# An attention kernel's instruction order from a table of sequences instead of a list scheduler

## The chip, the core and the metric

The kernel runs on one core of a Trainium2 chip. The metric is the device time of one execution in microseconds, as the median of several runs. The engines of the core run their own instruction queues in program order and meet at semaphores: TensorE (PE in the profile, with PEld its weight loads), VectorE (DVE), ScalarE (ACT), GpSimd (POOL) and SyncE (SP), which here only issues DMA transfers.

## The reference

Two attention blocks over a sequence of 2048 tokens, width 1024, 32 heads of 32, are computed and concatenated. Block A is plain softmax attention:

```python
qkv = (lambda x, *d: x.transpose(*d))((x @ wqkv).reshape(B, S, 3, H, Dh), 2, 0, 3, 1, 4)
q, k, v = (qkv[0], qkv[1], qkv[2])
scores = jnp.einsum('bhqd,bhkd->bhqk', q, k) * Dh ** (-0.5)
p = _softmax(scores, axis=-1)
o = jnp.einsum('bhqk,bhkd->bhqd', p, v)
return (lambda x, *d: x.transpose(*d))(o, 0, 2, 1, 3).reshape(B, S, D) @ wo
```

Block B works on four segments of 512 tokens in turn: causal softmax attention inside the segment, and beside it a linear-attention read of a memory that the segments before have filled. The two are mixed by a sigmoid gate per head and projected by a matrix of its own. All inputs are bf16, and so is the output of 1 x 2048 x 2048.

## The kernel before

Everything is in SBUF once, and the work is cut into 11,109 small operations, each with its engine, its dependencies and an estimated duration. Python code plans them first and emits them afterwards, engine by engine, in the order that a scheduler found.

*Scores and exponentials.* Heads go in eight groups of four, queries in chunks of 256. A row of scores (`plan_set`, matmuls at L1271, 32-row tiles, so four heads at once) fills two of three PSUM slots of two banks each. There are 592 rows, numbered here 0 to 591 in the order in which they are planned; no change of order touches that. Each slot is then read by an exponential on ScalarE (`plan_exp`, L1347; the first eight, with a bias, L1334), which writes bf16 to a ring of 20 P buffers. For 238 slots ScalarE takes one bank only, and VectorE evicts the other (Y, L1308), whose square GpSimd makes (Pc, L1311).

*Values and sums.* P and Pc are multiplied with the values (L1438) and with ones for the softmax sums (L1445) on 32-column tiles. A group is four matmuls of 256 columns, which run side by side on four tiles. They accumulate in two pool banks. VectorE normalizes (L1504 to L1521), GpSimd multiplies (L1570), and the result goes out to be transposed by a DMA.

*Projections.* All projections are jobs (`plan_jobs`) of eight steps, issued by one helper (L899). A step is four matmuls of 512 columns. It exists as two halves of 256 columns; `join` makes one step of two halves that stand next to each other on TensorE's queue.

*Guards.* Before a group of heads is used for the first time a bound on its scores is worked out, since the exponentials are free of a running maximum: squares (GpSimd, L1672), sums on TensorE (L1685, L1715), a maximum on VectorE (L1692, L1719), a diagonal (L1702), its spreading on TensorE (L1762), and on VectorE L1770, `braw` (L1776), `bias` (L1789) and `flags` (L1783). ScalarE loads the flag and branches on it before the first exponential that relies on it. At a second guard of the same group L1736 keeps a running maximum, and L1742 is the exponential of a bias difference on ScalarE.

*The order.* `Prog.schedule` (L509 to L715) is a list scheduler. It keeps the ready operations of each engine and takes the next one in simulated time: on TensorE by a rank (`pick`) in which a score row goes first when it is due, a value group by its place relative to the exponentials opened so far, and a job by its due time; on the other engines by key. Some thirty constants weigh these rules, and the table `SHIFT` adds a correction to the key of hundreds of single items. It also chooses which of the two pool banks a value group or a job takes, and adds to large DMA transfers a dependency on an exponential that has ended. The queue that it builds is the program order of the engine.

Of the kernel before, what the change touches and what calls it, by code (L numbers as in the profile page):

```python
# [24 lines left out]
OL_LEAD, OL_MAX = 3.567283411686441, 21.60561264796846  # L25
# [14 lines left out]
SOON = 0.5969023125738563  # L40
# [88 lines left out]
class Op:  # L129
# [4 lines left out]
    def __init__(self, eng, fn, dur, lat, key, mode=None, sem=None):  # L134
# [16 lines left out]
SWITCH = 0.1  # L151
WIN = 3.413
ROW_LEAD = 5.053495059459838
AHEAD = 1.6055122421540051
HEAT = 8.05297032017043
STICK = 3.256770423473878
OVER = 17.394741454160474
PV_ROOM = 6.408007584666841
PV_T = 1.0806361081944706
PV_HOT = 1.0883878031673944  # L160
NORM_K = 6.738
JOB_AT = 1.5887710826754966
JOB_SLOPE = 1.1413237083257293
# [3 lines left out]
LEAD_A, LEAD_B, DUE_AT, DUE_SLOPE = 10.658, 3.249, 7.018517831572489, 1.9480960937294671  # L167
HOLD = {}
BACKLOG = 3.378
XR = 70.3728830950375  # L170
XC = 5.80397040345515
# [4 lines left out]
SAFE = 0.0  # L176
SHIFT = {((f, n), e): v for f, e, t in (
# [10 lines left out]
    ("plan_constants", "ACT", {  # L188
        1: 15.5}),
    ("plan_constants", "POOL", {  # L190
# [114 lines left out]
    ("plan_prologue", "PE", {  # L305
        2: 1.5, 5: -3.25, 6: 12, 7: 5, 8: 17.25, 9: 0.5}),
    ("plan_prologue", "POOL", {
        3: 5.5, 8: 0.5}),
    ("plan_prologue", "SP", {
        4: 13.47, 10: -1.78}),  # L310
    ("plan_pv", "DVE", {
# [2067 lines left out]
```

## Time and profile before

| | us |
|---|---|
| median of 3 runs | 1045.36 |
| lowest and highest | 1044.49, 1045.73 |
| span of the profiled execution | 1044.3 |
| TensorE busy | 1019.2 |
| ScalarE busy | 1016.3 |
| VectorE busy | 700.4 |
| GpSimd busy | 585.5 |

The profiled execution's own time is not listed apart from its span; the span leaves out about 1.1 us of what the median of the runs has. Start times are counted from the start of the span. In a row of the timeline the first number is the start, the second the duration, and the brackets hold the idle time of the engine just before and the operation whose end released it.

### The profile page before, as it was taken

The numbers are of one execution on the slowest core, as the hardware profiler recorded it, in microseconds if no ns is written. First come the engines' busy times: TensorE is split into PE (matmuls) and PEld (weight loads), VectorE is DVE, ScalarE is ACT, GpSimd is POOL, SyncE is SP. The second block draws the span as 40 slices with busy tenths as digits, with TensorE's granted clock in tenths as the row PEclk, the third lists the DMA queues.
The fourth block names the chain that finished last, engine by engine and source line by source line (L and its number), as shares of the span: only waits on it lengthen the run. The fifth ranks groups of instructions, "written<-read, shape, count | busy, mean of one in ns | idle before, by whom it ended". The sixth has DMA issues, their size and how long they took to land.

```text
span 1044.3 us, 56017 instructions
## 1 busy us (share of the span) xinstructions
PE 1019.2 (98%) x25384; PEld 559.9 (54%) x25385; DVE 700.4 (67%) x1559; ACT 1016.3 (97%) x1225; POOL 585.5 (56%) x677
## 2 busy tenths in 40 slices
PE   8999999999999999999999999999999999999998
PEld 4555555655555555565555545565555545455554
DVE  3366676767566686887865687687755885874444
ACT  5999989999999999999999999999999999999997
POOL 2125476668645675766656476665644775653310
PEclk9999999999999999999999999999999999999999
DMA  9042352124313331033223320133113561021101
GB/s 210 15 96 54 78 130 36 20 38 106 80 42 92 80 79 34 11 99 51 71 58 94 98 60 18 28 92 54 51 29 87 174 171 25 24 79 57 59 24 59
DMA packets 171390, 72.17 MB, mean 69 GB/s; under 512 B 134800, under 2 KB 169360, under 8 KB 171152
## 3 DMA queue, kind: packets, MB, share of 16 engines
q1 hardware_dynamic: 168784, 67.79, 26.7%
q8 instruction: 200, 3.28, 1.3%
q10 hardware_dynamic: 2368, 0.79, 0.3%
q14 instruction: 38, 0.31, 0.1%
HBM read 45.29 MB, written 11.73 MB: 55 GB/s over the span
## 4 chain that ended last, share of the span: by engine, by line
PE 66%; ACT 29%; DVE 3%; issue 1%; DMA 1%; POOL 0%; ACTq 0%; DVEq 0%
PE ps L899 32%; ACT P L1347 28%; PE ps L1271 13%; PE ps L1438 9%; PE ps L1445 9%; PE ps L1964 1%; DMA xT_A<-in_A_x_dram 1%; ACT PKQ_B L2008 1%; DVE Y L1308 1%; DVE T L1508 0%; PE ps L1715 0%; DVE OT_B L2035 0%; DVE T L1510 0%; DVE KQ_B L1658 0%; PE ps L1814 0%
## 5 line engine op out<-in xcount | busy, mean ns | idle before, releaser
L1347 ACT ACTIVATE P<-ps 128x1024 bf16<-128x1024 f32 (+1 forms) x1176 | 988.4, 1059 | 9.8 <-PE ps L1271 3.2
L1311 POOL TENSOR_TENSOR Pc<-Y 128x512 bf16<-128x512 f32 x238 | 249.4, 1049 | 257.2 <-PE ps L899 79.3
L1445 PE MATMUL ps<-P,onesb 128*32 128x256 bf16 (+1 forms) x4388 | 295.9, 270 | 0.8 <-issue 0.7
L1438 PE MATMUL ps<-P,V_A 128*32 128x256 bf16 x3620 | 252.7, 274 | 0.4 <-DVE V_A L1974 0.3
L1308 DVE TENSOR_SCALAR Y<-ps 128x512 f32<-128x512 f32 x238 | 163.4, 686 | 97.7 <-PE ps L1271 83.8
L1271 PE MATMUL ps<-KQ_A 32*128 32x256 bf16 x4096 | 204.0, 273 | 7.4 <-ACT P L1347 5.7
L1271 PEld LDWEIGHTS ps<-KQ_A 32*128 32x128 bf16 x4096 | 62.0, 92 | 154.0 <-ACT P L1347 111.7
L1445 PEld LDWEIGHTS ps<-P,onesb 128*32 128x32 bf16 x4388 | 128.8, 96 | 25.9 <-issue 12.9
L899 PE MATMUL ps<-xT_A,W_A 128*32 128x512 bf16 (+1 forms) x2236 | 138.8, 363 | 2.3 <-DMA xT_A<-in_A_x_dram 1.2
L899 PE MATMUL ps<-xT_B,W_B 128*32 128x512 bf16 (+1 forms) x2284 | 139.0, 359 | 1.2 <-DVE KQ_B L1658 0.3
L1438 PEld LDWEIGHTS ps<-P,V_A 128*32 128x32 bf16 x3620 | 107.7, 96 | 26.2 <-issue 10.9
L1438 PE MATMUL ps<-Pc,V_A 128*32 128x256 bf16 x476 | 119.5, 273 | 0.2
L1445 PE MATMUL ps<-Pc,onesb 128*32 128x256 bf16 x476 | 119.6, 274 | 0.0
L1370 POOL TENSOR_SCALAR_AFFINE_SELECT P<-P 128x768 bf16<-128x768 bf16 (+1 forms) x96 | 75.7, 794 | 49.9 <-ACT P L1347 48.3
L1672 POOL TENSOR_TENSOR sqA<-KQ_A 128x512 bf16<-128x512 bf16 x61 | 64.0, 1061 | 60.9 <-PE ps L899 31.5
L1672 POOL TENSOR_TENSOR sqB<-KQ_B 128x512 bf16<-128x512 bf16 x64 | 68.4, 1070 | 24.9 <-DVE KQ_B L1658 19.0
L899 PEld LDWEIGHTS ps<-xT_B,W_B 128*32 128x32 bf16 x2284 | 53.2, 96 | 46.6 <-issue 17.1
L899 PEld LDWEIGHTS ps<-xT_A,W_A 128*32 128x32 bf16 x2236 | 52.0, 96 | 48.7 <-issue 17.1
L1521 DVE STREAM_TRANSPOSE T<-rc 128x256 f32<-128x256 f32 (+1 forms) x152 | 72.3, 479 | 2.6
L899 PE MATMUL ps<-Wv_B,xT_B 128*32 128x512 bf16 (+1 forms) x1124 | 71.0, 362 | 0.8 <-issue 0.7
L1658 DVE CAST KQ_B<-ps 128x512 bf16<-128x512 f32 x64 | 44.1, 688 | 39.1 <-PE ps L899 38.4
L899 PE MATMUL ps<-Wo_B,OT_B 128*32 128x512 bf16 (+1 forms) x1112 | 68.6, 364 | 0.3 <-DVE T L1504 0.2
(117 smaller groups left out, 1224.5 us busy)
## 6 DMA issues: line engine op xcount, KB each, us to landing
Wv_B<-in_B_wv_dram SPq DMA_DIRECT2D x32, 256.0 KB, 3.3
W_B<-in_B_wk_dram SPq DMA_DIRECT2D x32, 256.0 KB, 3.4
W_B<-in_B_wq_dram SPq DMA_DIRECT2D x32, 256.0 KB, 4.0
Wo_B<-in_B_wo_dram SPq DMA_DIRECT2D x32, 256.0 KB, 3.3
out_dram<-outsb SPq DMA_DIRECT2D x56, 128.0 KB, 1.9
W_A<-in_A_wqkv_dram SPq DMA_DIRECT2D x14, 256.0 KB, 3.4
ot_a_scratch<-OTst SPq DMA_DIRECT2D x51, 64.0 KB, 1.8
xT_A<-ot_a_scratch SPq DMA_DIRECT2D x6, 512.0 KB, 4.9
```

The lines of the kernel that those rows point to most:

```text
L899: ins = e.matmul(out[r], w[:, r], x, start=start, stop=stop, tile_position=(0, 32 * t), skip_group_check=True)
L1271: ins = e.matmul(out, kap, qap, start=st, stop=True, tile_position=(32 * h, 0), skip_group_check=True)
L1308: o = self.dve(lambda e: e.tensor_scalar(Y[:, :], src, KAPPA * SCALE, BETA, ALU.mult, ALU.add), 512, key - 9.0, [self.bank[bank]], [rY], f ...
L1311: last.append(self.pool(lambda e: e.tensor_tensor(dst, Y[:, :], Y[:, :], ALU.mult), 512, key - BCK, [rY], [rP], rate=0.56))
L1347: a = self.act(guarded if early else lambda e: e.activation(dst, src, ACT.Exp, scale=SCALE), cols, key, rd, wr, fixed=EXP_FIXED + (0.095 i ...
L1370: self.pool(lambda e: e.affine_select(v, v, pattern=pat, compare_op=ALU.is_ge, fill=0.0, base=0, channel_multiplier=-1), 2 * nd * P, key + ...
L1438: ins = e.matmul(self.pb(obk, q0, q0 + nq, slice(32 * h, 32 * h + 32)), v, p, start=first, stop=last, tile_position=(0, 32 * h), skip_grou ...
L1445: ins = e.matmul(self.pb(obk, QC + q0, QC + q0 + nq, slice(32 * h, 32 * h + 32)), self.onesb[:, 0:32], p, start=False, stop=last, tile_pos ...
L1521: self.dve(lambda e: e.transpose(L2.rearrange("p (b r) -> p b r", r=32), bc), n, key, [rr], [rl], fixed=0.17)
L1658: self.dve(lambda e: e.tensor_copy(dst, src()), 512, key, [self.at(b)], rdst, fixed=0.155)
L1672: self.pool(lambda e: e.tensor_tensor(sq[:, :], src, src, ALU.mult), 512, key, [rsrc], [rs], rate=0.56)
L1964: o = self.pe(lambda e, i=i, t=t, k=k: e.matmul(self.pb(b, P * k, P * k + P), self.xT[:, i, P * t:P * t + P], self.WAv[:, i, P * half:P * ...
```

## The change

`SHIFT` and the constants of the list scheduler are gone. A table `ORDER` holds for each engine the sequence of its operations as pairs of a jump and a run length over the planned operations. `schedule` builds the queues from it and replays all engines to get start and end times, the pool bank that is free first and the dependencies of large transfers. One more line lets an exponential depend on the operation that writes its flag, which before only the branch did. The operations are the same. Behind the new function all lines have a number 27 or 28 higher than before (so L1271 is L1298 in the order after, L899 L926, L1438 L1466, L1445 L1473, L1789 L1817, L1783 L1811).

```diff
-SHIFT = {((f, n), e): v for f, e, t in (
-    ("load_OT_early", "SP", {
-        0: 5.57}),
...
+ORDER = {
+    "PE": (
+        25, 15, 13, 21, 7, 1, -8, 3, 117, 1, -111, 1, 3, 9, 118, 1, -119, 7, 118, 1, -105, 10, 7, 16, -23, 6, 114, 1,
...
     def schedule(self):
...
+        queue = {}
+        for e, runs in ORDER.items():
+            at, q = 0, []
+            for jump, n in zip(runs[::2], runs[1::2]):
+                at += jump
+                q += self.ops[at:at + n]
+                at += n
+            assert all(o.eng == e for o in q)
+            queue[e] = q
...
-        def pick(t, av, c):
-            mode = st["mode"]
-            row = [x for x in av if x.urgent]
...
+        def opening(b):
+            if holder[b] is not None and holder[b].left or not done.issuperset(last[b]):
+                return 1e9
+            return max((x.end + x.lat for x in last[b]), default=0.0)
...
+            for e, q in queue.items():
+                if at[e] == len(q):
+                    continue
+                o = q[at[e]]
...
+                if o.svc >= 0.8:
+                    was = next((x for x in reversed(progs) if x.end <= t), None)
+                    if was is not None:
+                        o.deps.add(was)
...
             if not early:
                 a.alt, a.flag = alt, self.flag_of[bc]
+                a.deps.add(a.flag[1])
```

Out of the longest common sequence of the two orders stand 957 operations of TensorE, 550 of VectorE, 267 of GpSimd, 175 of SyncE and 26 of ScalarE. Score rows and exponentials keep their own sequence. 117 steps more than before are issued as two halves, 468 matmuls more; changes of TensorE between 32-row and 32-column tiles are 1194 in place of 1198. The 238 evictions Y stand earlier in VectorE's queue, the normalizations later. Three places follow; in each row stand the line, the instruction, what it writes and reads, the size, and how many such instructions follow each other.

On VectorE, the guard of block B's first keys, at 142 us of the trace; T_2 is a normalization's tile and cu its correction. Before:

```order
L1464 TENSOR_SCALAR cu<-corr,flags 128x1 x2
L1719 TENSOR_REDUCE ps<-ps 128x1
L1702 TENSOR_SCALAR dg<-ps 128x32
L1770 TENSOR_REDUCE cols<-ps 128x2
L1776 TENSOR_SCALAR braw<-cols 128x1
L1504 TENSOR_TENSOR T_2<-ps,cu 128x512
L1789 TENSOR_SCALAR bias<-braw 128x1
L1783 TENSOR_SCALAR flags<-braw,flags 128x1
L1506 STREAM_TRANSPOSE T_2<-T_2 128x256
```

And after:

```order
L1534 STREAM_TRANSPOSE T_1<-T_1 128x256
L1547 RECIPROCAL rc<-T_1 128x8
L1747 TENSOR_REDUCE ps<-ps 128x1
L1730 TENSOR_SCALAR dg<-ps 128x32
L1798 TENSOR_REDUCE cols<-ps 128x2
L1804 TENSOR_SCALAR braw<-cols 128x1
L1817 TENSOR_SCALAR bias<-braw 128x1
L1811 TENSOR_SCALAR flags<-braw,flags 128x1
L1492 TENSOR_SCALAR cu<-corr,flags 128x1 x2
L1532 TENSOR_TENSOR T_2<-ps,cu 128x512
```

The subtraction into T_2 (L1504, now L1532) and the two corrections cu have moved behind the flag; two steps of another normalization now stand ahead of the guard.

On TensorE, from score row 182 on, around 327 to 332 us of the trace; KQ_A rows are score rows, xT_B,W_B and xT_A,W_A projection steps, P,V_A and P,onesb value and sum groups. Before (behind these rows come two more steps and four more groups, then row 185):

```order
L1271 MATMUL ps<-KQ_A 128x256 x8
L899 MATMUL ps<-xT_A,W_A 32x256 x4
L899 MATMUL ps<-xT_A,W_A 32x512 x16
L899 MATMUL ps<-xT_B,W_B 32x512 x20
L1271 MATMUL ps<-KQ_A 128x256 x8
L899 MATMUL ps<-xT_B,W_B 32x512 x24
L1271 MATMUL ps<-KQ_A 128x256 x8
L899 MATMUL ps<-xT_B,W_B 32x512 x12
L1438 MATMUL ps<-P,V_A 32x256 x4
L1445 MATMUL ps<-P,onesb 32x256 x4
```

And after, from row 182 to row 185:

```order
L1298 MATMUL ps<-KQ_A 128x256 x8
L926 MATMUL ps<-xT_A,W_A 32x512 x20
L926 MATMUL ps<-xT_B,W_B 32x512 x4
L1298 MATMUL ps<-KQ_A 128x256 x8
L926 MATMUL ps<-xT_B,W_B 32x512 x20
L1298 MATMUL ps<-KQ_A 128x256 x8
L926 MATMUL ps<-xT_B,W_B 32x512 x40
L926 MATMUL ps<-Wv_B,xT_B 32x256 x4
L1298 MATMUL ps<-KQ_A 128x256 x8
```

Each row from 183 on has fewer projection steps ahead of it, and the eight groups that stood between rows 184 and 185 have moved behind row 185.

On TensorE again, from row 433 to row 434, around 762 to 764 us. Before:

```order
L1271 MATMUL ps<-KQ_A 128x256 x8
L1438 MATMUL ps<-P,V_A 32x256 x4
L1445 MATMUL ps<-P,onesb 32x256 x4
L1438 MATMUL ps<-P,V_A 32x256 x4
L1445 MATMUL ps<-P,onesb 32x256 x4
L899 MATMUL ps<-xT_B,W_B 32x512 x8
L899 MATMUL ps<-xT_B,W_B 32x256 x4
L1271 MATMUL ps<-KQ_A 128x256 x8
L899 MATMUL ps<-xT_B,W_B 32x256 x4
L899 MATMUL ps<-xT_B,W_B 32x512 x20
```

And after:

```order
L1298 MATMUL ps<-KQ_A 128x256 x8
L926 MATMUL ps<-xT_B,W_B 32x512 x12
L926 MATMUL ps<-xT_B,W_B 32x256 x4
L1466 MATMUL ps<-P,V_A 32x256 x4
L1473 MATMUL ps<-P,onesb 32x256 x4
L1466 MATMUL ps<-P,V_A 32x256 x4
L1473 MATMUL ps<-P,onesb 32x256 x4
L926 MATMUL ps<-xT_B,W_B 32x256 x4
L926 MATMUL ps<-xT_B,W_B 32x512 x16
L1298 MATMUL ps<-KQ_A 128x256 x8
L1466 MATMUL ps<-P,V_A 32x256 x4
L1473 MATMUL ps<-P,onesb 32x256 x4
```

The whole projection job of eight steps now stands between the two rows, where two and a half of its steps did, and value groups follow row 434 at once.

More of the change, by code (lines that the diff above doesn't have):

```diff
@@ L166 @@
 RX0 = 34.374
[L167 to L168 removed]
+LEAD_A, LEAD_B = 10.658, 3.249
 BACKLOG = 3.378
[L170 to L171 removed]
 STEP = 1.599
@@ L549, in schedule @@
+        for q in queue.values():
+            for n, o in enumerate(q):
+                o.pos = n
+        for o in self.ops:
+            assert all(x.eng != o.eng or x.pos < o.pos for x in o.order)
+        at = dict.fromkeys(queue, 0)
+        free = dict.fromkeys(queue, 0.0)
+        ready = dict.fromkeys(queue)
         last = {b: list(r.w) + list(r.r) for b, r in self.before.items()}
         holder = dict.fromkeys(last)
-        st = self.st = dict(mode=None, prog=0.0, act_end=0.0, recent=[], win=0, acts={}, slow=0.0, opn=0, dma=0.0,
-                            rows=sum(o.urgent is not None and o.eng == "PE" for o in self.ops))
+        acts, win, low, mode, held, dma = {}, 0, False, None, 0.0, 0.0
@@ L559, in ready_of @@
                         (TO_POOL if o.eng == "POOL" and x.eng == "DVE" else 0.0) +
                         (TO_DVE if o.eng == "DVE" and x.eng == "PE" else 0.0))
-            for x in o.order:
-                t = max(t, x.start)
-            for x, w in o.gate:
-                t = max(t, x.end + x.lat - w)
-            return t
-        def past(t):
-            return next((x for x in reversed(queue["ACT"]) if x.prog and x.end <= t), None)
-        def opens(o):
-            return o.grp is not None and o is o.grp.pe[0]
```

235 lines of the change are left out of this document (46 added, 189 removed), and 666 rows, old and new, of tables (ORDER, SHIFT).

## The prediction

> **What bounds the kernel now.** I read the page first, then the waits of ScalarE, then ScalarE's busy time by stretch, then the timeline around each idle stretch that this showed.
>
> ```profile
> span 1044.3 us, 56017 instructions
> PE 1019.2 (98%) x25384; PEld 559.9 (54%) x25385; DVE 700.4 (67%) x1559; ACT 1016.3 (97%) x1225; POOL 585.5 (56%) x677
> PE 66%; ACT 29%; DVE 3%; issue 1%; DMA 1%; POOL 0%; ACTq 0%; DVEq 0%
> L1347 ACT ACTIVATE P<-ps 128x1024 bf16<-128x1024 f32 (+1 forms) x1176 | 988.4, 1059 | 9.8 <-PE ps L1271 3.2
> ```
>
> Two engines look full. The chain lies on TensorE for two thirds, but a full PE is modelled; what tells more is who waits. The exponentials (L1347) keep ScalarE busy for 988.4 us, and all its idle time in front of them is 9.8 us. TensorE's score rows (L1271) wait the other way:
>
> ```profile
> PEld ps L1271 <- ACT P L1347: 133.8, 416, 1.5
> PEld ps L1271 <- DVE Y L1308: 21.5, 67, 0.6
> ```
>
> So 483 times a row stood ready and its PSUM slot was not yet free. ScalarE sets the pace, and TensorE is a close second: 133.8/416 is 0.32 us a wait. Turning from the other tile shape costs 0.21 even for a row that waits for nothing:
>
> ```profile
> 333.50 0.12 PEld L1271 LDWEIGHTS ps<-KQ_A 32*128 32x128 bf16 x8 [0.21 <-issue]
> ```
>
> So a waiting row has on average about 0.1 us to spare. The change reorders the same work. It can give back ScalarE's idle time and no more, so I price it idle stretch by idle stretch. ScalarE's busy time by stretch, from the end of the start-up on:
>
> ```profile
> 24.00:140.00 116.00, 115.73 (x143) 1.00 0.31 66
> 140.00:145.00 5.00, 2.09 (x4) 1.00 0.56 168
> 145.00:333.00 188.00, 187.64 (x231) 1.00 0.29 67
> 333.00:335.00 2.00, 1.11 (x3) 1.00 0.00 0
> 335.00:396.00 61.00, 60.50 (x73) 1.00 0.30 73
> 396.00:398.00 2.00, 1.27 (x2) 1.00 0.34 66
> 398.00:765.00 367.00, 366.15 (x441) 1.00 0.25 59
> 765.00:767.00 2.00, 0.70 (x2) 1.00 0.00 0
> 767.00:1036.60 269.60, 268.64 (x321) 1.00 0.25 72
> 1036.60:1044.30 7.70, 1.20 (x2) 1.00 0.25 82
> ```
>
> Between 24 and 1036.6 us the idle time adds up to 0.27+2.91+0.36+0.89+0.50+0.73+0.85+1.30+0.96 = 8.77 us. The 7.7 us at the end are the last projection and its stores. The granted clock is 1.00 in every stretch, so no term hangs on the clock.
>
> The large ones by name, from the timeline (in brackets the idle time before the first exponential of a run):
>
> ```profile
> 143.82 1.02 ACT L1347 ACTIVATE P<-ps 128x1024 bf16<-128x1024 f32 x1 [2.91 <-PE ps L899]
> 333.95 1.94 ACT L1347 ACTIVATE P<-ps 128x1024 bf16<-128x1024 f32 x2 [0.89 <-PE ps L1271]
> 397.09 1.02 ACT L1347 ACTIVATE P<-ps 128x1024 bf16<-128x1024 f32 x1 [0.73 <-PE ps L1271]
> 766.46 2.43 ACT L1347 ACTIVATE P<-ps 128x1024 bf16<-128x1024 f32 x3 [1.30 <-PE ps L1445]
> 300.45 1.94 ACT L1347 ACTIVATE P<-ps 128x1024 bf16<-128x1024 f32 x2 [0.21 <-PE ps L1445]
> 760.90 4.26 ACT L1347 ACTIVATE P<-ps 128x1024 bf16<-128x1024 f32 x5 [0.18 <-PE ps L1271]
> ```
>
> These six are 6.22 us of the 8.77; the other 2.55 us are in small pieces.
>
> **The change, part by part.** *The guard at 143 us.* The first is no wait for a matmul, whatever the bracket says: ScalarE branches on a flag that VectorE writes at L1783.
>
> ```profile
> 142.30 0.21 DVE L1776 TENSOR_SCALAR braw<-cols 128x1 f32<-128x1 f32 x1
> 142.43 0.68 DVE L1504 TENSOR_TENSOR T<-ps,cu 128x512 f32<-128x512 f32 x1
> 143.03 0.21 DVE L1789 TENSOR_SCALAR bias<-braw 128x1 f32<-128x1 f32 x1
> 143.15 0.21 DVE L1783 TENSOR_SCALAR flags<-braw,flags 128x1 f32<-128x1 f32 x1
> ```
>
> The flag ends at 143.36, and the exponential follows 0.46 us later, after the flag is loaded and branched on. In the new order the 0.68 us subtraction (L1504) stands behind the flag. L1789 can then start 0.25 us behind L1776 (142.55; the same distance separates L1776 and L1783 in the next fence) and L1783 0.12 later, at 142.67 in place of 143.15: −0.5 us. Its bounds are 0, if TensorE or the transposes now put ahead of the chain hold it back, and −0.7, the whole subtraction.
>
> *The start.* The same chain for the second guard:
>
> ```profile
> 21.14 0.24 DVE L1702 TENSOR_SCALAR dg<-cols 128x32 bf16<-128x32 f32 x1
> 22.06 0.17 DVE L1770 TENSOR_REDUCE cols<-ps 128x2 f32<-128x16 f32 x1 [0.49 <-PE ps L1762]
> 22.27 0.21 DVE L1776 TENSOR_SCALAR braw<-cols 128x1 f32<-128x1 f32 x1
> 22.52 0.22 DVE L1783 TENSOR_SCALAR flags<-braw,flags 128x1 f32<-128x1 f32 x1
> 23.42 1.94 ACT L1347 ACTIVATE P<-ps 128x1024 bf16<-128x1024 f32 x2 [1.06 <-PE ps L1964]
> ```
>
> The diagonal is ready at 21.38, but VectorE waits 0.49 us for the spreading matmul L1762, which stands behind a score row; now it stands ahead of that row: −0.3. The bias (L1789) now comes before the flag: +0.13. The correction factor's exponential (L1742) moves from behind five exponentials into this wait, which costs nothing there. Together −0.2, bounds −0.5 and +0.3. Two weight loads go ahead of two transposing loads on SP's queue, and the transposes land later by them; ScalarE waits for neither here, so 0, and up to +1 if the projection behind them is.
>
> *Work moved behind rows that came late.* I count TensorE's work ahead of a row in the two orders and price it by the distance of starts on the full engine:
>
> ```profile
> 1035.00 0.28 PE L1438 MATMUL ps<-P,V_A 128*32 128x256 bf16 x4
> 1035.11 0.28 PE L1445 MATMUL ps<-P,onesb 128*32 128x256 bf16 x4
> 1035.22 1.04 PE L899 MATMUL ps<-V_A,xT_A 128*32 128x512 bf16 x16
> 1036.08 0.39 PE L899 MATMUL ps<-W_A,xT_A 128*32 128x512 bf16 x4
> 762.19 0.40 PE L1271 MATMUL ps<-KQ_A 32*128 32x256 bf16 x8
> ```
>
> A group of four 256-wide matmuls is 0.11; sixteen 512-wide ones take 0.65 longer than four, so a whole step of four is 0.22, and a half step 0.11. From row 182 to row 185, whose exponential is the one at 333.95, there were 20 steps, a half and eight groups, 5.4 us; now there are 21.5 steps, 4.7 us: −0.7, bounds 0 (VectorE's Y, which frees a slot there, stays as late) and −0.9. The same count for rows 220 to 223 gives −0.55 at 397.09 (bounds 0 and −0.7). At 766.46 the exponential waits until the value matmuls have read its P buffer. Work ahead of that last read is 0.4 less, and those eight groups now follow row 434 directly, so the read ends earlier still; but row 434 itself has 1.0 us more ahead of it, since seven steps and two halves now stand between rows 433 and 434 where there were two and a half. The old read and the new row then decide in turn; I take −0.5, bounds −0.9 and +0.4. The groups ahead of 300.45 and the row at 760.90 have 2.0 and 0.7 us less ahead, more than their idle time: −0.4 for both.
>
> *Small idle time.* Of the 2.55 us I take a third back, −0.9, my choice, since the trace does not say which of these rows had late work that moved; bounds 0 and −2.
>
> *Rows that get more work ahead.* By the same count nine rows have 0.3 to 1.0 us more: 434, 298, 304, 250, 187, 94, 516, 55 and 112, 5.7 us in all. A row is issued when the exponential of an earlier slot frees its banks; one more exponential (1.06 on the page) stands in front of ScalarE then, and the row takes 0.40, so 0.66 us is covered. Row 434 is in the term above already; 298, 304 and 250 (0.9, 0.8, 0.7) exceed it by 0.4 together, and I add as much again for rows whose cover is shorter: +0.8, bounds 0 and +4.6.
>
> *Steps issued in halves.* 117 more steps are issued as two 256-wide halves, 468 more matmuls, and changes between row and column tiles stay the same but for four. By the rows above two halves (2 × 0.11) take as long as a whole (0.22): 0. [...]
>
> *VectorE and GpSimd.* The 238 evictions Y (L1308) and their squares come earlier in their queues, the softmax normalizations later. What waits for the former is TensorE's row, which has its slot sooner; what waits for the latter is the output projection, far ahead of its due time. No idle stretch of ScalarE but 333.95 has such an end, so 0. The new dependency of exponentials on their flag adds no wait that the branch did not have. The end: the same projection steps behind the last exponential, one more value group of 0.11 beside them: 0.
>
> Sum: −0.5 −0.2 −0.7 −0.55 −0.5 −0.4 −0.9 +0.8 = −2.95. The profiled execution spans 1044.3 and its time lies beside the median of 1045.36 (1044.49 to 1045.73) with about 1.1 us outside the span: 1041.4 of span, 1042.4 us of time.
>
> **The rivals.** *The idle time only moves.* TensorE has little room, and work pushed behind row 185 stands in front of row 187, whose count rises by 0.6. For it: the 0.1 us of slack above. Against it: 483 rows still wait for a slot, so there is room a few rows on. Only the guards' −0.7 stay: 1044.7.
>
> *Slower: work ahead of just-in-time rows.* If the cover of 0.66 is not there, because a row's first exponential is the next that ScalarE takes, the nine rows' 5.7 us count from 0.1 of slack each: 5.7 − 0.9 = +4.8, and the gains from moved work go with it. 1045.4 − 0.7 + 4.8 = 1049.5. It decides from the point where a row starts more than 0.1 us behind the freeing of its slot; the 8 idle stretches behind L1271 that ScalarE shows in all of 592 rows speak against it:
>
> ```profile
> ACT P L1347 <- PE ps L1271: 3.2, 8, 0.9
> ```
>
> *Halves cost.* If each split leaves one weight load in the open, the row below gives 117 × 0.096 = 11.2 us of TensorE time, 1053.6 with the other terms, and less where rows wait anyway. The starts above speak against it.
>
> ```profile
> L899 PEld LDWEIGHTS ps<-xT_B,W_B 128*32 128x32 bf16 x2284 | 53.2, 96 | 46.6 <-issue 17.1
> ```
>
> [...]
>
> *All idle time goes.* The order is fitted closely enough that exponentials never wait after 24 us: 1045.4 − 8.8 = 1036.6. Against it, the guard at 143 keeps over two of them by the count above.
>
> *The table only restates the old order.* Excluded: 957 operations of TensorE and 550 of VectorE are out of the old sequence.
>
> **How the numbers follow.** Forecast 0.54, idle time only moves 0.24, slower 0.14, halves cost 0.03, all goes 0.05. The forecast is 1042.4 us. Its terms' bounds, not all at one end together, give about 1039.5 to 1045; the range reaches below for part of the case in which more idle time goes and above into the slower one: 1038.5 to 1047.5. A measurement of this kernel can tell about 0.2%, 2.1 us, from no change: faster is below 1043.3. Of the forecast's 0.54 some 0.46 lies there, with the 0.05 and 0.03 of the second case: 0.54. Slower than 1047.4: 0.14 and 0.03 less their mild part, 0.15. The rest, 0.31, is no difference.
>
> **What would show it.** In the profile after: the idle time before the exponential near 143 falls from 2.91 to about 2.4 with L1504 behind the flag; the stretches at 333, 397 and 766 fall to 0.2, 0.2 and 0.8; ScalarE's busy time stays 1016; four half-step matmuls stay 0.11 apart. Wrong would be: new idle stretches of over 0.3 us in front of rows 298, 304, 250 or 434 (the slower case), idle time of the same sum at other rows (it only moves), or more TensorE time in L899 with starts of halves over 0.12 apart.

## The result and the profile after

The kernel after takes 1057.57 us (median of 4 runs, 1053.38 to 1059.21), the one before 1045.55 beside it (1044.49 to 1045.76). The ratio is 1.0107, with a 95% interval of 1.0085 to 1.0128: slower by about 12 us, where 3 us less were forecast. The runs of the new order also lie further apart, 5.8 us against 1.3.

From the page of the kernel after, its span, the engines' busy time and the exponentials, whose line is now L1374:

```profile
span 1056.1 us, 56857 instructions
PE 1023.6 (97%) x25853; PEld 572.3 (54%) x25853; DVE 698.0 (66%) x1559; ACT 1017.2 (96%) x1225; POOL 584.4 (55%) x677
L1374 ACT ACTIVATE P<-ps 128x1024 bf16<-128x1024 f32 (+1 forms) x1176 | 987.8, 1056 | 20.3 <-PE ps L1298 14.9
```

ScalarE's work is the same, 987.8 us of exponentials against 988.4. Its idle time in front of them has more than doubled, 9.8 to 20.3. The table of waits says for whom (total, times, longest):

```profile
ACT P L1374 <- PE ps L1298: 14.9, 15, 5.2
PE ps L926 <- issue: 4.5, 4, 2.8
PE ps L926 <- DVE outsb L1686: 3.8, 1, 3.8
```

Score rows cost ScalarE 14.9 us where they cost 3.2. TensorE's projections (L926) waited once for 3.8 us for a cast of the output, a row that the table of before does not have. They also waited four times for nothing that the profile names ("issue"), 4.5 us in all and once for 2.8; before, that row was 1.0 us in two waits. ScalarE's busy time by stretch (length, then busy time and count, granted TensorE clock, share and rate of the DMA; the share adds up packets that overlap, so it can pass 1):

```profile
24.00:475.00 451.00, 444.25 (x539) 1.00 0.27 62
475.00:486.00 11.00, 6.59 (x9) 0.84 1.20 192
486.00:606.00 120.00, 120.00 (x147) 1.00 0.21 52
606.00:618.00 12.00, 5.38 (x7) 0.72 0.25 61
618.00:1047.90 429.90, 427.39 (x512) 1.00 0.25 68
```

Idle time from 24 us to the last exponential is 6.75 + 4.41 + 0 + 6.62 + 2.51 = 20.29 us; it was 8.77. The span is 24 us, 1003.62 of work, 20.29 idle and 8.2 behind it, 1056.1 in all; before, 24, 1003.83, 8.77 and 7.7. So the loss is idle time, and all but half a microsecond of it (11.03 of 11.52) lies in two stretches of 11 and 12 us. Outside them the new order is as good as the old one, not better.

**The places that the forecast named.** The timeline of the kernel after around 143, 333, 397 and 766 us (in brackets the idle time before the first of a run):

```profile
142.45 0.20 DVE L1811 TENSOR_SCALAR flags<-braw,flags 128x1 f32<-128x1 f32 x1
143.06 0.69 DVE L1532 TENSOR_TENSOR T<-ps,cu 128x512 f32<-128x512 f32 x1
143.14 4.69 ACT L1374 ACTIVATE P<-ps 128x1024 bf16<-128x1024 f32 x5 [2.10 <-DVE cu L1492]
333.23 3.52 ACT L1374 ACTIVATE P<-ps 128x1024 bf16<-128x1024 f32 x4 [0.26 <-PE ps L1298]
337.05 2.86 ACT L1374 ACTIVATE P<-ps 128x1024 bf16<-128x1024 f32 x3 [0.30 <-PE ps L1298]
396.36 10.38 ACT L1374 ACTIVATE P<-ps 128x1024 bf16<-128x1024 f32 x12
776.37 3.42 ACT L1374 ACTIVATE P<-ps 128x1024 bf16<-128x1024 f32 x4 [0.28 <-PE ps L1298]
```

The subtraction stands behind the flag, and 2.91 us have become 2.10. At 333 us 0.89 are 0.26; at 397 there is no idle time; the 1.30 at 766 are four pieces, none over 0.28. The second guard's exponential, at 23.42 us before, is at 22.56.

**The first new stretch, 475 to 486 us.** SP's queue, TensorE and ScalarE there (a row of SP's queue, SPq, is the issue on the engine, not the transfer):

```profile
469.39 6.11 SPq L1651 DMA_TRANSPOSE xT_B<-in_B_x_dram  x1
477.96 1.27 PE L926 MATMUL ps<-Wv_A,xT_A 128*32 128x256 bf16 x34 [2.78 <-issue]
480.68 1.51 ACT L1374 ACTIVATE P<-ps 128x512 bf16<-128x512 f32 x2 [3.46 <-PE ps L1298]
483.15 1.02 ACT L1374 ACTIVATE P<-ps 128x1024 bf16<-128x1024 f32 x1 [0.95 <-PE ps L1298]
```

TensorE stops for 2.78 us between the second and the third matmul of a step, where the profile names nothing that it waits for. A late block of its instructions fits this. The page counts the blocks of code that came in during the kernel:

```profile
q8 instruction: 203, 3.33, 1.3%
```

By this row they are 16.4 KB each (3.33 MB over 203), one about every 5 us; 51,706 matmuls and weight loads over 203 blocks are some 255 a block. The kernel before has 200 blocks for 50,769, some 254. In the DMA records of the trace one block starts at 467.58 us and the next only at 475.54. Between them lies the transposing load of x: its issue on SP runs from 469.39 to 475.50, and its data have landed at 479.09. TensorE had started 410 instructions since the last fetch when it stopped at 474.91; it goes on 2.4 us after the next one starts. In the old order SP issues the same load at 455.63, in front of four weight loads, with fetches at 455.14 and 460.88, and TensorE does not stop.

The clock falls behind the pause. TensorE by stretch, the granted clock ahead of the DMA's two columns:

```profile
478.00:480.00 2.00, 2.00 (x50) 0.72 1.32 259
480.00:482.00 2.00, 2.00 (x34) 0.50 1.33 223
482.00:484.00 2.00, 2.00 (x52) 0.93 0.95 181
```

The columns are averages over 2 us. The trace has a clock of either 1.0 or 0.5, and it is halved from 478.88 to 482.29 us, 3.41 us. A pause of 2.78 us and that stretch together became 4.41 us on ScalarE. In e2 and e4 below, pauses of 1.71 and 1.98 us were followed by the same 3.41 us at half clock. The length of the pause does not decide it alone: in e8 one of 2.26 us at 489.67 us was followed by full clock.

**The second, 606 to 618 us.** The cast of one output tile on VectorE, SP's queue up to its store (L2119), then VectorE, TensorE and ScalarE:

```profile
542.86 0.69 DVE L1686 CAST outsb<-ps 128x512 bf16<-128x512 f32 x1 [1.70 <-PE ps L1466]
601.54 2.66 SPq L1651 DMA_TRANSPOSE PKt_B<-PKQ_B  x1
605.34 0.58 SPq L2119 DMA_DIRECT2D out_dram<-outsb  x1
609.47 0.69 DVE L1686 CAST outsb<-ps 128x512 bf16<-128x512 f32 x1 [4.65 <-DMA out_dram<-outsb]
610.22 0.83 PE L926 MATMUL ps<-xT_B,W_B 128*32 128x512 bf16 x8 [3.83 <-DVE outsb L1686]
612.50 1.02 ACT L1374 ACTIVATE P<-ps 128x1024 bf16<-128x1024 f32 x1 [5.21 <-PE ps L1298]
615.88 2.43 ACT L1374 ACTIVATE P<-ps 128x1024 bf16<-128x1024 f32 x3 [1.42 <-PE ps L1473]
```

This is a chain over four engines. The output tile that was cast at 542.86 us is stored only at 605.34, 62 us later, because the new order puts its store that far back on SP's queue, behind loads, a transposing load and a store of OTst. In the order before, the store of the same tile follows its cast, which ends at 538.06, at once:

```profile
538.09 0.62 SPq L2091 DMA_DIRECT2D out_dram<-outsb  x1
```

There are three outsb buffers. In the new order the next cast into this one, at 609.47 us, waits 4.65 us until the store has landed, at 609.45. That cast holds a PSUM bank, TensorE waits 3.83 us for the bank, and the rows behind it come 5.21 us late. The clock is halved here as well, from 608.59 to 615.41 us.

### The profile page after: what moved, and what is told of

Read it like the earlier page. It is cut to its first block, busy times and chain, and to the rows that moved or that the text cites. A ratio compares the mean times of both kernels' runs of the same rounds, so it can differ in the third digit from the quotient of the medians.

```text
span 1056.1 us, 56857 instructions
## 1 busy us (share of the span) xinstructions
PE 1023.6 (97%) x25853; PEld 572.3 (54%) x25853; DVE 698.0 (66%) x1559; ACT 1017.2 (96%) x1225; POOL 584.4 (55%) x677
## 3 DMA queue, kind: packets, MB, share of 16 engines
q1 hardware_dynamic: 168784, 67.79, 26.5%
q8 instruction: 203, 3.33, 1.3%
## 4 chain that ended last, share of the span: by engine, by line
PE 59%; ACT 34%; DVE 2%; DMA 2%; issue 2%; POOL 0%; SPq 0%; ACTq 0%; DVEq 0%
ACT P L1374 34%; PE ps L926 29%; PE ps L1298 12%; PE ps L1466 9%; PE ps L1473 8%; PE ps L1992 1%; DMA W_B<-in_B_wq_dram 1%; DMA xT_A<-in_A_x_dram 1%; DVE Y L1335 1%; ACT PKQ_B L2036 1%; DMA out_dram<-outsb 0%; PE ps L1743 0%; DVE PKQ_B L2042 0%; DVE T L1536 0%; DVE outsb L1686 0%
## 5 line engine op out<-in xcount | busy, mean ns | idle before, releaser
L1374 ACT ACTIVATE P<-ps 128x1024 bf16<-128x1024 f32 (+1 forms) x1176 | 987.8, 1056 | 20.3 <-PE ps L1298 14.9
L1473 PE MATMUL ps<-P,onesb 128*32 128x256 bf16 (+1 forms) x4388 | 300.6, 271 | 0.1
L1466 PE MATMUL ps<-P,V_A 128*32 128x256 bf16 x3620 | 259.1, 275 | 0.1
L1298 PE MATMUL ps<-KQ_A 32*128 32x256 bf16 x4096 | 204.4, 273 | 8.2 <-ACT P L1374 4.0
L926 PE MATMUL ps<-xT_B,W_B 128*32 128x512 bf16 (+1 forms) x2356 | 145.3, 356 | 7.3 <-DVE outsb L1686 3.8
L926 PE MATMUL ps<-xT_A,W_A 128*32 128x512 bf16 (+1 forms) x2408 | 146.1, 349 | 1.3 <-DMA xT_A<-in_A_x_dram 0.9
L1298 PEld LDWEIGHTS ps<-KQ_A 32*128 32x128 bf16 x4096 | 62.0, 92 | 152.6 <-ACT P L1374 103.1
L1473 PEld LDWEIGHTS ps<-P,onesb 128*32 128x32 bf16 x4388 | 129.1, 97 | 25.3 <-issue 13.1
L1466 PEld LDWEIGHTS ps<-P,V_A 128*32 128x32 bf16 x3620 | 107.8, 96 | 29.4 <-issue 12.2
L1466 PE MATMUL ps<-Pc,V_A 128*32 128x256 bf16 x476 | 121.0, 274 | 0.0
L1473 PE MATMUL ps<-Pc,onesb 128*32 128x256 bf16 x476 | 120.7, 274 | 0.1
L926 PEld LDWEIGHTS ps<-xT_B,W_B 128*32 128x32 bf16 x2356 | 55.6, 96 | 52.3 <-issue 20.3
L926 PEld LDWEIGHTS ps<-xT_A,W_A 128*32 128x32 bf16 x2408 | 57.4, 96 | 43.5 <-issue 16.4
L926 PE MATMUL ps<-Wv_B,xT_B 128*32 128x512 bf16 (+1 forms) x1200 | 74.3, 351 | 0.4 <-DVE T L1532 0.3
L926 PE MATMUL ps<-Wo_B,OT_B 128*32 128x512 bf16 (+1 forms) x1220 | 72.7, 346 | 0.1
L1686 DVE CAST outsb<-ps 128x512 bf16<-128x512 f32 x56 | 38.4, 686 | 50.1 <-PE ps L926 28.4
```

What stands on the lines that cost most here:

```text
L926: ins = e.matmul(out[r], w[:, r], x, start=start, stop=stop, tile_position=(0, 32 * t), skip_group_check=True)
L1298: ins = e.matmul(out, kap, qap, start=st, stop=True, tile_position=(32 * h, 0), skip_group_check=True)
L1374: a = self.act(guarded if early else lambda e: e.activation(dst, src, ACT.Exp, scale=SCALE), cols, key, rd, wr, fixed=EXP_FIXED + (0.095 i ...
L1466: ins = e.matmul(self.pb(obk, q0, q0 + nq, slice(32 * h, 32 * h + 32)), v, p, start=first, stop=last, tile_position=(0, 32 * h), skip_grou ...
L1473: ins = e.matmul(self.pb(obk, QC + q0, QC + q0 + nq, slice(32 * h, 32 * h + 32)), self.onesb[:, 0:32], p, start=False, stop=last, tile_pos ...
L1686: self.dve(lambda e: e.tensor_copy(dst, src()), 512, key, [self.at(b)], rdst, fixed=0.155)
```

## The experiments

Theory A: SP's new order of DMA issues, which the forecast had priced at nothing, makes both stretches. Its rivals: B, the new function itself (its choice of PSUM banks and its added dependency) costs the time whatever the order is; C, the added halves cost it; D, TensorE has no room, and idle time taken away at one row comes back at others. Several edits below move one issue (or operation) in front of another, just ahead of the numbering of the queues, in this form:

```diff
+        for e, o, x in (("SP", 5786, 6516),):
+            q = queue[e]
+            q.remove(self.ops[o])
+            q.insert(q.index(self.ops[x]), self.ops[o])
```

**e1, the old order as a table.** The new function, with the table filled from the sequences that the old scheduler made.

> The order of before on all five engines, put into the new table and replayed by the new function. Theory A (two stalls that come from SyncE's new order of DMA issues): 1045 us, within 1 us of before, since SyncE's order is the old one. Rival B (the new function itself costs: its choice of pool banks, the added dependency of exponentials on flags): 1050 us or more with the old order too.

1046.66 us (1044.76 to 1047.82), ratio 1.0011 (1.0001 to 1.0020), span 1044.5. By the interval B costs 0.1 to 2.1 us, 1.0 by the medians of the ratios, and falls as the cause of 12: the loss is in the order.

**e2, the load of x ahead of the weight loads; e3, the output store put out earlier; e4, both.** The edits are the form above with ("SP", 4957, 5088), with ("SP", 5786, 6516), and with both.

> The changed kernel with one DMA issue moved: the transposing load of block B's third segment (469.39 in the profile after) goes ahead of the four value-weight loads and the store that stood before it, as it stood before the change. Theory A (TensorE's code fetch is held up by that transposing load when it comes on top of the loads): no idle stretch near 480, its 3.46 and 0.95 us go, about 1053 us. Rival C (the code is longer by 468 matmuls and its fetches run dry by themselves): the stretch stays or comes back nearby, 1057 us.

> The changed kernel with one DMA issue moved: the output store of 605.34 goes four places ahead, before the load and the transpose at 601. Theory A (VectorE's cast at 609 waits for that store, TensorE for the cast): the idle stretches of 5.21 and 1.42 us at 612 and 616 go, about 1051 us. Rival D (the cast waits for something else that the profile puts on the store, or another store is next): 1055 us or more.

> The changed kernel with both moves. Theory A: both stalls gone, 11 us less than the profile after, 1046 to 1047 us: what is left is the new order of the computing engines alone, whose gains and losses in the profile after nearly cancel. Rival E (the computing engines' order costs by rows that come just in time): 1050 us or more.

e3: 1050.95 (1050.36 to 1052.91), ratio 1.0045 (1.0028 to 1.0062), 6.6 us below the kernel after by the medians, about what the stretch held. ScalarE in e3 over the same two places:

```profile
470.00:490.00 20.00, 18.25 (x23) 1.00 0.97 188
604.00:628.00 24.00, 23.73 (x29) 1.00 0.55 136
```

One store moved four issues up leaves 0.27 us of idle time where 6.62 were. The chain from the store to the row is shown. That the two figures agree to 0.1 us is in part chance: the profiled run of e3 is its slowest, its span is 4.9 us below that of the kernel after, and it has more idle time and work elsewhere.

e2 is a miss: 1060.63 (1056.08 to 1063.94), ratio 1.0137 (1.0101 to 1.0172), no faster than the kernel after. So is e4: 1052.30 (1050.71 to 1054.24), ratio 1.0057 (1.0037 to 1.0077), where 1046 to 1047 were expected. The pause for code did not go, it moved. In e4:

```profile
458.75 4.51 SPq L1655 DMA_TRANSPOSE xT_B<-in_B_x_dram  x1
466.42 0.19 PE L1794 MATMUL ps<-pick,dg 128*32 128x16 bf16 x4 [1.98 <-issue]
467.69 2.02 ACT L1378 ACTIVATE P<-ps 128x1024 bf16<-128x1024 f32 x2 [1.63 <-PE ps L1302]
```

In e2 fetches start at 456.67 and 463.34 us, with the load between them from 458.13 to 462.59 and 425 instructions started meanwhile; TensorE then stops for 1.9 us. So the load's place ahead of the weight loads is not enough: there, too, a fetch comes late beside it.

**e6, no transposing load there; f3, the load late in the old order.** e6 is e3 with the third load of x brought in as one plain block of 128 KB; the other three quarters of it are left out. f3 is the old order with the load moved behind the four weight loads, where the new order has it.

```diff
+        if s == 2:
+            self.dma(lambda e: e.dma_start(self.xTB[:, 0, :], xb[L * s:L * s + P, 0:L]), ...
+            return
         self.turn(self.xTB[:, :, :], xb[L * s:L * s + L, :], self.sm_xTB, key, [], [self.r_xTB], 5.0, 3.4, True)
```

> The changed kernel with the output store moved ahead as in the run before, and the transposing load of block B's third segment replaced by a plain load of 128 KB into the same tile, so that segment is computed from mostly stale input. Theory A (the transposing load holds up TensorE's code fetch): the fetch after 470 comes within 5 us of the one before, the idle stretches of 1.33 and 0.26 us near 481 go, 1049 to 1050 us beside 1051 for the store move alone. Rival C (the code is too dense there whatever the DMA does): a pause of TensorE of 1.5 to 3 us near 478 stays.

> The old order with one DMA issue moved: the transposing load of block B's third segment goes behind the four value-weight loads that it stood before. Theory A: it takes 5 to 6 us in place of 3.8 and holds the code fetch so long that TensorE pauses 1 to 3 us near 465 to 475; 1046.5 to 1049 us. Rival G (the pause needs the new order's denser code): no pause over 0.7 us there, 1045 to 1046 us.

e6: 1049.50 (1048.39 to 1051.18), ratio 1.0039 (1.0026 to 1.0052). Its medians do not tell it from e3, but its profile shows the place. ScalarE in e6:

```profile
24.00:470.00 446.00, 438.68 (x531) 1.00 0.26 60
470.00:490.00 20.00, 19.92 (x26) 1.00 0.65 142
490.00:1038.40 548.40, 545.77 (x655) 1.00 0.24 65
```

With the transposing load gone the fetch comes in time, and 0.08 us are left of e3's 1.75. This fits theory A and does not prove it: in g2 and g3 below, with the load where e3 has it, only 0.34 and 0.54 us are left there. The block is also a plain load with a quarter of the bytes, so e6 could not tell transposing from bytes. f3: 1045.42 (1044.32 to 1048.39), ratio 1.0004 (0.9995 to 1.0013). In it the load runs from 466.99 to 472.47, a fetch starts at 469.12 and is not held, and TensorE does not stop. So the late load alone is harmless here. Which fetches are held beside such a load and which pass, the runs do not settle: in g2 and g3 fetches started 3.25 and 3.43 us behind its issue, and TensorE has no pause of over 0.41 us there.

**e5, more halves in the old order; f2, halves rejoined in the new.** e5 leaves 237 whole steps of the old order as halves, 948 matmuls more, twice what the change adds. f2 is e3 with 237 split steps joined.

```diff
+        apart = {self.ops[n] for n in APART}
...
-            if a.both is not None and a.both[0] is b:
+            if a.both is not None and a.both[0] is b and a not in apart:
```

> The old order on every engine, with the 237 steps that the change splits issued as two halves each: 948 matmuls more, twice the net of the change, and nothing moved. Rival C (halves cost TensorE time, 0.1 us a split): 1045 and up to 24 us more, with starts of halves over 0.12 us apart. Theory A (two halves take as long as a whole; they only make the code longer): 1045 to 1047 us, starts 0.11 apart, and pauses of TensorE without a semaphore only where a transposing load falls together with dense code.

> The changed kernel with the output store moved ahead, and in the 237 steps that the change splits the second half moved up to stand right behind the first, so that they are issued whole: 948 matmuls fewer. Theory A with the code's density as part of it (shorter code gives the fetch more time): the pauses at 477 and 876 shrink, 1048 to 1050 us beside 1051. Rival F (the halves are placed where they fit, and work that moves up makes rows late): 1052 us or more.

e5: 1048.47 (1046.45 to 1049.67), ratio 1.0024 (1.0015 to 1.0033), 1.8 us over e1 by the medians. f2: 1051.08 (1050.70 to 1051.83), ratio 1.0058, no better than e3. The change's 468 matmuls would thus cost about 0.9 us by e5, and f2 could not show even that. C falls as the cause. Over 948 matmuls e5's 1.8 us would be an estimated 1.9 ns each. The runs do not tell that from the cost of the more code that e5 fetches, an estimated seven blocks (1,896 matmuls and weight loads at 255 a block).

**e7 and e8, one engine's queue from the other order.** e7 has the new order with SP's old sequence, e8 the old order with SP's new one. The queues would block each other, so 38 and 14 of SP's issues are taken out of turn.

> The new order on the four computing engines with SyncE's old order, in which 38 issues are taken out of turn where the new order of the others needs it. Theory A (what is lost comes from SyncE's issues): no stall on the output store at 606, pauses of TensorE's code fetch as before the change or shorter, 1045 to 1048 us. Rival E (the computing engines' new order loses by itself): 1050 us or more with no wait for a DMA. Some of the issues taken out of turn may wait themselves; the trace shows it then as a wait for a load.

> The old order on the four computing engines with SyncE's new order, in which 14 issues are taken out of turn. Theory A: slower than before by stalls on DMA or on the code fetch, 1050 us or more. Rival E (SyncE's order does not matter): 1045 to 1047 us.

1148.74 us (ratio 1.0996) and 1063.97 (ratio 1.0171, 1.0156 to 1.0187). e7 misses the 1045 to 1048 us expected of it by 100 us; e8 falls on the side of theory A. Both are confounded by the issues out of turn and separate nothing; they show the price of a misfit. In e8 stores of OTst wait on SP's queue, GpSimd waits for their buffers, and an exponential at 152.82 us for 10.8 us:

```profile
POOL OTst L1581 <- DMA ot_a_scratch<-OTst: 29.2, 7, 9.6
ACT P L1357 <- DVE cu L1475: 10.8, 1, 10.8
```

**f1 and f4, the new order in front, the old behind.** f1 takes the new order to 75 us and the guard's subtraction behind its flag, f4 the new order to 440 us; the tables are spliced there.

> The new order of all engines for what starts in the first 75 us, the old order from there on, and of the later changes one alone: at the guard of 143 us VectorE's subtraction (L1504) stands behind the flag. The profiles show exponentials 0.8 to 1.5 us earlier at 70 us in the new order, and the guard's idle stretch 0.7 us shorter. If both hold by themselves: 1043.5 to 1044 us, 1.5 to 2 us faster than before. If an idle stretch only moves: 1045 to 1046.

> The new order of all engines for what starts in the first 440 us, the old order from there on: it has the guard, the rows of 333 and 397 and the start, and neither stall. The forecast's terms for this part are 0.5, 0.2, 0.7, 0.55 and half of the 0.4, some 2.1 us: 1043.5 us. If the idle time only moved: 1045 to 1046.5 us.

1049.10 (ratio 1.0039, 1.0026 to 1.0052) and 1051.15 (ratio 1.0069, 1.0051 to 1.0088). Both miss, since the splice itself waits: idle stretches of 1.95 and 0.71 us at 83 and 85 us in f1, of 2.32, 0.78 and 0.68 at 455 to 460 in f4. What the new order does ahead of the splice is better read in the kernel after itself. From 24 to 400 us, the kernel before, the kernel after and f4:

```profile
24.00:400.00 376.00, 370.36 (x453) 1.00 0.30 68
24.00:400.00 376.00, 370.35 (x452) 1.00 0.29 67
24.00:400.00 376.00, 368.64 (x449) 1.00 0.29 68
```

The gains at 143, 333 and 397 us are in it, and the new order has 5.65 us of idle time there against 5.64: what it wins by then it has also lost. The 7.36 us of f4 have in them what a pause of TensorE for code cost, 1.22 us at 209.44, which the kernel after does not have there.

**g1, three of the forecast's moves alone in the old order.** The subtraction behind its flag, row 185 ahead of the work that stood before it, and the value groups of 766 us half a job forward.

```diff
+        for e, o, x in (("DVE", 1578, 1579), ("PE", 3664, 3620), ("PE", 8240, 7801), ("PE", 8241, 7801), ...
```

> The old order, with three of the moves that the forecast counted on and nothing else: VectorE's subtraction (L1504) behind the flag at 143 us, row 185 ahead of the two groups and five steps of work that stood in front of it, and the value groups that the exponential at 766 us waits for put half a job further forward. SP's order, the halves and all other rows stay as they were. Theory A (the forecast's gains at these places are real and are kept to the end if nothing else is moved; the new order loses by its DMA issues, by VectorE's other work in front of Y and by the longer code of TensorE): idle time at 143, 333 and 766 falls by 0.5, 0.6 and 0.5, and the time comes out 1.0 to 2.0 us below the old order written as a table, about 1044.0 to 1045.5 where the kernel before gives 1045.5. Theory B (TensorE has no room, so that idle time taken away at one row comes back at later rows): the three stretches fall, but the sum of ScalarE's idle time stays within 0.4 us, and the time is that of the old order as a table, 1046 to 1047.

1047.17 (1046.23 to 1049.19), ratio 1.0023 (1.0014 to 1.0032), against 1.0011 for e1: no gain, with intervals that overlap. ScalarE in g1 at the two places on TensorE:

```profile
333.79 1.94 ACT L1358 ACTIVATE P<-ps 128x1024 bf16<-128x1024 f32 x2 [0.39 <-PE ps L1282]
337.17 2.44 ACT L1358 ACTIVATE P<-ps 128x512 bf16<-128x512 f32 x3 [1.44 <-PE ps L1282]
768.16 1.51 ACT L1358 ACTIVATE P<-ps 128x512 bf16<-128x512 f32 x2 [0.17 <-PE ps L1282]
770.98 2.47 ACT L1358 ACTIVATE P<-ps 128x1024 bf16<-128x1024 f32 x3 [1.31 <-PE ps L1282]
```

Both places gain (0.89 to 0.39, where 0.7 were forecast, and 1.30 to 0.17, where 0.5 were), and the next rows lose 1.44 and 1.31, with the work put behind the first row now in front of them. This is D for single moves, at a price of one row for another. It is not pure: TensorE also waits 0.75 us for a Y of VectorE at 333.34 us and 0.47 for a cast of KQ_B at 768.58, operations that the new order had moved forward too. In the whole new order the row behind 333 us lost 0.30.

**g2 and g3, VectorE's order in front of two of the new stretches.** Both are e3 with two operations of VectorE moved as well. In the kernel after, VectorE, TensorE and ScalarE ahead of the stretch at 96 us:

```profile
92.79 1.07 DVE L1598 TENSOR_TENSOR OTst<-OT_B,T 128x256 bf16<-128x256 f32 x1
93.89 0.89 DVE L1935 CAST gc<-graw 32x8 f32<-32x8 bf16 x1
94.81 0.69 DVE L1335 TENSOR_SCALAR Y<-ps 128x512 f32<-128x512 f32 x1
95.65 0.40 PE L1298 MATMUL ps<-KQ_A 32*128 32x256 bf16 x8 [1.54 <-DVE Y L1335]
96.09 1.02 ACT L1374 ACTIVATE P<-ps 128x1024 bf16<-128x1024 f32 x1 [1.37 <-PE ps L1298]
```

g2 moves ("DVE", 1094, 794) and ("DVE", 4916, 4906), g3 moves ("DVE", 1082, 743) and ("DVE", 4906, 4885).

> The new order with the output store put out as early as in the third experiment, and two evictions Y of VectorE moved forward: the one for the exponential at 96 us ahead of the normalization and the cast that the new order puts in front of it, and the one for the exponential at 454 us ahead of the clearing of Zb and a cast. Theory A (these two stretches are VectorE's order and nothing else): idle time at 96 us falls from 1.37 to under 0.4 and at 454 us from 0.7 to under 0.3, and the time comes out 1.5 to 2 us below the third experiment's 1051.0, about 1049 to 1049.5. Theory B (what is won at a row is lost within the next hundred microseconds, since TensorE's work is the same): the two stretches go, and the time stays at 1050.5 to 1051.5. Against both: a pause of TensorE's code at another place can move the time by 1 to 2 us either way, and would show as a gap in the middle of a step.

> g2_store_y had moved the wrong rows of VectorE: the Y that the row at 96 us waits for is the one behind the product OTst and the cast gc, and at 457 us TensorE's step with PKQ_B waits for the cast of KQ_A, not for Y. Here, beside the early output store, that Y stands ahead of the OTst product, and the clearing of Zb stands behind the cast and the Y. Theory A (both stretches are VectorE's order in front of what TensorE waits for): idle time at 96 us falls from 1.37 to under 0.5 and at 457 us from 0.67 to under 0.3, together 1.2 to 1.7 us; if no pause for code comes in their place the time is 1049 to 1050 where the store alone gave 1050.95. Theory B (the work of the stretch is only put off, as in g1_local, where the time won at rows 185 and 435 was lost at the next one): new idle time of over 0.5 us within ten rows of each place, and the time stays at 1050.5 to 1052.

g2: 1053.54 (1052.31 to 1054.82), ratio 1.0081. It had moved the wrong rows, and ScalarE's wait of 2.24 us at 100.50 us for VectorE's cast gc came on top. g3: 1050.42 (1049.83 to 1052.83), ratio 1.0059 (1.0044 to 1.0073), no better than e3. At 457 us (454 in the kernel after), where TensorE waits for a cast of KQ_A behind the clearing of Zb, the idle time is gone; at 96 us it has moved 2.3 us on:

```profile
96.71 1.26 PE L930 MATMUL ps<-xT_B,W_B 128*32 128x512 bf16 x20 [0.94 <-DVE KQ_A L1690]
98.83 0.21 ACT L1941 ACTIVATE gc<-gc 128x8 f32<-128x8 f32 x1 [1.39 <-DVE gc L1939]
```

With Y early, the cast of KQ_A is late for TensorE, and the cast gc late for ScalarE. This suggests that VectorE has too much to do between 92 and 99 us in the new order; no run moved its work out of there.

## Why the prediction was wrong

*The named gains came, and most sizes held.* The guard at 143 gave 0.81 us (0.5 forecast), the start 0.86 (0.2), row 185 0.63 (0.7), 397 us 0.73 (0.55), 766 us 0.44 (0.5), and the stretches at 300 and 761 us, 0.39 together (0.4), are gone. That is 3.9 us. The guard and the start came out beyond their bounds of 0.7 and 0.5. The start was mis-sized, because the wait for the spreading matmul and the first factor's exponential both left the chain.

*The step that failed is the price of SP's queue.* The prediction weighed it at the start only ("so 0, and up to +1") and put the rest of its 175 moved issues at nothing without a reason; the list of waits of before, by which it priced, cannot show what a new order will make wait. The new SP order holds a store back for 62 us that went out at once before, for 6.62 us of idle time on ScalarE (shown by e3). It also puts loads where TensorE's code comes late beside them, for 4.41 us at 477. That the code was late is seen in the traces, and that this was the load of x is argued from them: the late fetch has the load beside it in the kernel after, e2, e3 and e4, and without the load (e6) there is no pause, but with it g2 and g3 have next to none. These 11.0 us are most of the 15.2 between the forecast and the result. With them the premise failed that the change "can give back ScalarE's idle time and no more", and also "no term hangs on the clock": it was halved behind the first stall and from within the second on.

*A second step failed in the same way, with a smaller price:* "No idle stretch of ScalarE but 333.95 has such an end, so 0", for VectorE. Its new order has part in new stretches of 1.37 us at 96 and 0.73 at 454, 2.1 us together (g3: the second goes, the first moves on).

*"Small idle time, −0.9" failed too.* Outside the two stretches idle time is 9.26 us, against 8.77: 3.0 us of the gains lie in this stretch of time, and 3.5 net were lost against them. Beside the two stretches of VectorE these are 0.65 at 351, 1.03 at 885, and others of 0.2 to 0.3. TensorE ahead of the ones at 351 and 885:

```profile
349.46 1.16 PE L926 MATMUL ps<-xT_B,W_B 128*32 128x512 bf16 x20 [0.68 <-DMA W_B<-in_B_wq_dram]
884.03 0.94 PE L926 MATMUL ps<-xT_B,W_B 128*32 128x512 bf16 x16 [1.21 <-issue]
```

Both point at SP's order again, but only by the traces. At 349 us TensorE waits for a weight load that SP issued at 344.61, where the old order issued it at 342.94. At 884 us TensorE stops 2.3 us behind a late fetch of code (881.71, the one before at 873.75) with no transposing load near, but with plain loads that keep the DMA's share at 1.05 from 877 to 885 us. All nine traces with SP's new order behind 440 us have such a pause between 874 and 887 us, of 0.59 to 1.60 us. Of the others none has one of 0.45 us or more there; before and f1 have one of 0.67 and 0.64 at 845 and 850 us. No run moved one of these loads.

*The rival "the idle time only moves"* had the right sum, but mostly by other causes than its own. The place that it named, row 187, lost 0.30 us (337.05). Its mechanism is shown for single moves by g1, and its 1044.7 us had no queue of SP in it.

*"Rows that get more work ahead, +0.8".* Of the nine rows, 187 lost 0.30 and 434 lost 0.28, which is in the 0.86 left at 766; the others have no new stretch of their own. The cover of 0.66 us was there and the term is about 0.3 here; the slower rival's mechanism did not occur. That the outcome lies on its side is no support for it.

*"Steps issued in halves, 0"* should have been about 0.9 us with e5's size, inside the noise of these runs. The busy time of ScalarE did not quite stay at 1016, it rose by 0.9 to 1017.2 us, and the time behind the last exponential grew from 7.7 to 8.2 us.

*What stays open.* Without the store's stall and with the fetch at 477 in time (e6), the time is 8.1 of the 12 us lower by the medians. Its profiled run, the fastest of its runs, has a span of 1046.6 us: 1.26 us more idle time than before, 0.5 at the end and 0.5 of work. Its median is still 3.8 us over the kernel before. From kernel to kernel the pauses for code come at other places, and what makes up the rest was not measured.

## What to carry to other kernels

A reordering is priced on every queue that it touches, DMA issues above all: for each transfer moved, find the wait of the issue in front of it, the buffers its data hold, and who fills them next (one store moved in e3 was worth 6.6 us by the medians). An idle stretch of the bound engine taken away at one row can come back at the next, if the work pushed behind that row makes it late (g1: 0.89 us became 0.39, and 1.44 came 3.4 us later); count the next three rows as well. When an order was tuned by replaying engines, look for what the replay does not hold, here the instruction stream of TensorE, 3.33 MB that came by DMA beside 67.79 MB of data on the busiest queue.

## What the runs showed of the hardware

- TensorE's code came in blocks of 16.4 KB (203 of them, 3.33 MB), about 255 instructions, one about every 5 us. Two blocks came late in the kernel after, beside loads that kept the DMA busy: 7.96 us behind the last one beside the transposing load at 469 us (DMA share 1.07 from 469.4 to 475.5), and 7.96 beside plain loads at 881 us (1.05 from 877 to 885). TensorE then stopped and went on 2.2 to 2.9 us behind the start of the late fetch. In all traces but e7's the last holds for each of the 33 waits of 0.45 us or more behind 24 us that the profile puts on "issue"; 318 to 489 matmuls and weight loads had started since the fetch before. For its 203 blocks the kernel after's table of waits has four waits of TensorE on "issue", 4.5 us in all; the longest was 2.78 us.
- TensorE's clock in the trace of the kernel after was 1.0 or 0.5. Pauses for code of 2.78, 1.71 and 1.98 us (the kernel after, e2, e4) were each followed by 3.41 us at half clock; others of 2.26 us (e8), 1.63 (e2), 1.60 and 1.39 us (e3) were not. During the wait of 3.83 us for the cast, 2.5 us behind TensorE's last start, it fell to half and stayed there for 6.8 us.
- An output tile's store held its buffer until its place on SP's queue came: the store at 605 us went out 62 us behind its cast, and the next cast into that buffer waited 4.65 us; putting it four issues forward, 5 us earlier, gave back 6.6 us by the medians.
- 948 matmuls more, in halves, cost 1.8 us by the medians against the old order as a table, with intervals of about 1 us on each.
